# A maxout FFN behind local-window attention on one core: the output matmuls spread over the next chunk, two chunks of 256 tokens, another load order

## The chip, the core and the metric

The kernel runs on one core of a Trainium2 chip. A core has a matrix engine (TensorE, PE in the profile; its weight loads are shown apart as PEld), three engines for the rest (VectorE, DVE; ScalarE, ACT; GpSimd, POOL), and a queue engine that issues transfers (SyncE, SP). Each runs its own list of instructions in the order in which the program gave them, and waits for the others through semaphores. Data lie in SBUF, matmul results in the eight banks of PSUM. The metric is the device time of one execution in microseconds (us).

## The reference

There are 4 batches, 8 heads, 768 positions and head dimension 64. Each position sees the 96 last positions (itself included) and the first 8 positions of its sequence, with a bias that falls linearly with the distance. The attention output, 3072 tokens of 512 numbers, goes through a feed-forward network (FFN) with the maximum of three products:

```python
scores = scale * np.matmul(q, k.transpose(0, 1, 3, 2))
keep = is_global | is_local
dist = np.where(is_global & ~is_local, float(n_local), np.abs(rel).astype(np.float32))
scores = scores + (-slopes[:, None, None] * dist[None, :, :])[None, :, :, :]
scores = np.where(keep, scores, -1000000000.0)
a = np.exp(scores - np.max(scores, axis=-1, keepdims=True))
a = a / (np.sum(a, axis=-1, keepdims=True) + 1e-09)
x = np.matmul(a, v).transpose(0, 2, 1, 3).reshape(B * S, H * D)
h = np.maximum(np.maximum(x @ w1, x @ w2), x @ w3)   # 512 -> 768
return h @ w_out                                      # 768 -> 512
```

## The kernel before

The 3072 tokens are 24 tiles of 128 (six to a batch). Tile T is worked on in units, which are functions of the kernel:

- `load(T)` issues three transfers on SP (q, k, v of 256 KB each) into one of four buffers `raw`.
- `cast(T)` makes bf16 of q and k (L102) and of v (L104) on POOL. v stands in `va`, with a column of ones behind each head.
- `u_X(T)`, **X**: eight transposes on PE (L130) into the PSUM tile `tp`, and the copy to SBUF, `qkT`, on DVE (L132). Then POOL makes `kgT` (this tile's keys with the batch's first eight put in, L123 and L124) and `vg` (the same for v, L112 and L113), which the next tile uses as its second block of keys.
- `u_S(T, g)`, **S**, for half g of the heads: scores on PE into `sp` (L146), the exponential on ACT (L152, for the first tile of a batch L154). The product with the mask of biases, on DVE (L153, L155), is put off to the start of the next attention unit.
- `u_A(T, g)`, **A**: probabilities times v on PE into `op` (L166, L169); on DVE the reciprocal of the sum (L175) and the product with it (L176) into `xb`.
- `u_XT(T)`, **T**: four transposes of `xb` on PE into the same bank as `tp` (L187), and a copy on DVE into `xT` (L188).

The FFN goes by chunks of four tiles (512 tokens). `u_F1(c, f, j)`, **F1**, gives 128 of the 768 hidden numbers for product j: four matmuls into one bank `h0`, `h1` or `h2` (L199). For j = 0 ACT copies the bank (L204); for j = 1 and 2 DVE takes the maximum (L206, L208), the last into `ht`. `u_F2(c, tt)`, **F2**, gives the output of one tile: six matmuls into the bank `po` (L214), a copy on ACT into `ost` (L217), a store on SP (L219). A chunk is 18 F1 and then its four F2.

`load_w(g)` loads a third of the three weights (three transfers of 512 KB; here w0, w1, w2 for the groups), `cast_w(g)` makes bf16 of the three parts: w1's on ACT, w2's on DVE, w3's on POOL (L241 to L243).

What sets the order is the order in which the program emits units, and it is written by hand. The list `att` holds the attention units of all tiles. First `att` runs up to T(3), the last tile of chunk 0. Then, for each chunk c, F1 and F2 are emitted in turn, and between them the attention units of chunk c + 1, evenly. Per tile `att` has this order, which puts X of the next tile and T of the tile before side by side, and X(5) ahead of T(3):

```python
for i in range(NTT + 1):
    # S(i,0), A(i-1,1), S(i,1), X(i+1), T(i-1), A(i,0)
```

The loads are issued when the units ask for them, in the order tiles 0 to 3, w0, w1, w2, tile 4, w_out, tile 5, and on; X(T) asks for tile T + 3. Each of the PSUM tiles `tp`, `op`, `po`, `h0`, `h1`, `h2` is one bank and `sp` two; none has a second buffer.

Of the kernel before, what the change touches and what calls it, by code (L numbers as in the profile page):

```python
# [19 lines left out]
def kernel(  # L20
# [56 lines left out]
    NVA = 4  # L77
    va_ring = [persist.tile([128, H, 65], BF16, name=f"va{i}") for i in range(NVA)]
    va_first = [persist.tile([128, H, 65], BF16, name=f"vaf{i}") for i in range(2)]
    vg_ring = [persist.tile([128, H, 65], BF16, name=f"vg{i}") for i in range(3)]  # L80
    kg8 = [persist.tile([128, NP, NG], BF16, name=f"kg8_{i}") for i in range(2)]
# [4 lines left out]
    xT = {}  # L86
    va, vg = {}, {}

    def load(T):
# [7 lines left out]
    def cast(T):  # L97
        b, t = divmod(T, NT)
        r = raw[T]
        qk = cast_pool.tile([128, 2, DM], BF16, name="qkb", tag="qkb")  # L100
        qb[T] = qk
        nc.gpsimd.tensor_copy(qk, r[:, 0:2].rearrange("p a h d -> p a (h d)"))  # L102
        va[T] = va_first[b % 2] if t == 0 else va_ring[T % NVA]
        nc.gpsimd.tensor_copy(va[T][:, :, 0:D], r[:, 2])  # L104

    def make_vg(T):
        b, t = divmod(T, NT)
        if t == 0:
            vg[T] = va[T]
        elif t < NT - 1:  # L110
            vg[T] = vg_ring[T % 3]
            nc.gpsimd.tensor_copy(vg[T], va[T])  # L112
            nc.gpsimd.tensor_copy(vg[T][0:NG], va[b * NT][0:NG])  # L113

    def make_kg(T):
        b, t = divmod(T, NT)
        kT = qkT[T][:, 1]
        if t == 0:
            kgT[T] = kT
            nc.gpsimd.tensor_copy(kg8[b % 2], kT[:, :, 0:NG])  # L120
        elif t < NT - 1:
            kgT[T] = kg_pool.tile([128, NP, 128], BF16, name="kgT", tag="kgT")
            nc.gpsimd.tensor_copy(kgT[T], kT)  # L123
            nc.gpsimd.tensor_copy(kgT[T][:, :, 0:NG], kg8[b % 2])  # L124

    def u_X(T):
        tp = psT.tile([128, 2, NP, 128], BF16, name="tp", tag="tp")
        for a in range(2):
            for jp in range(NP):
                nc.tensor.transpose(tp[:, a, jp], qb[T][:, a, jp * 128:(jp + 1) * 128], identb)  # L130
        qkT[T] = qkT_pool.tile([128, 2, NP, 128], BF16, name="qkT", tag="qkT")
        nc.vector.tensor_copy(qkT[T], tp)  # L132
        make_kg(T)
        make_vg(T)
        return []

    def u_S(T, g):
        b, t = divmod(T, NT)
        sp = psS.tile([128, 2, 2, 2, 128], FP32, name="sp", tag="sp")
        for ds in range(2 if t else 1):  # L140
            for j2 in range(2):
                jp = 2 * g + j2
                for hh in range(2):
                    hsl = slice(64 * hh, 64 * hh + 64)
                    st = qkT[T][hsl, 1, jp] if ds == 0 else kgT[T - 1][hsl, jp]
                    nc.tensor.matmul(sp[:, hh, j2, ds], st, qkT[T][hsl, 0, jp],  # L146
                                     start=True, stop=True, skip_group_check=True)
        P = p_pool.tile([128, 4, 2, 128], BF16, name="P", tag="P")
        Pt[T, g] = P
        spv = sp.rearrange("p a b d n -> p (a b) d n")  # L150
        if t:
            nc.scalar.activation(P, spv, AF.Exp, bias=0.0, scale=scale)  # L152
            return [lambda: nc.vector.tensor_mul(P, P, wmask[:, g])]  # L153
        nc.scalar.activation(P[:, :, 0], spv[:, :, 0], AF.Exp, bias=0.0, scale=scale)  # L154
        return [lambda: nc.vector.tensor_mul(P[:, :, 0], P[:, :, 0], wmask0[:, g])]  # L155

    def u_A(T, g):
        b, t = divmod(T, NT)
        op = psO.tile([128, 4, 65], FP32, name="op", tag="op")
        P = Pt[T, g]  # L160
        for j2 in range(2):
            for hh in range(2):
                h = 4 * g + 2 * j2 + hh
                i = 2 * hh + j2
                o = op[:, 2 * j2 + hh]
                nc.tensor.matmul(o, P[:, i, 0], va[T][:, h], start=True, stop=(t == 0),  # L166
                                 skip_group_check=True)
                if t:
                    nc.tensor.matmul(o, P[:, i, 1], vg[T - 1][:, h], start=False, stop=True,  # L169
                                     skip_group_check=True)  # L170
        if g == 0:
            xb[T] = xb_pool.tile([128, H, D], BF16, name="xb", tag="xb")
        x = xb[T]
        rz = z_pool.tile([128, 4], FP32, name="rz", tag="rz")
        nc.vector.reciprocal(rz, op[:, :, 64])  # L175
        nc.vector.tensor_tensor(out=x[:, 4 * g:4 * g + 4], in0=op[:, :, 0:64],  # L176
                                in1=rz[:, :, None].to_broadcast([128, 4, D]), op=ALU.mult)
        return []

    def u_XT(T):  # L180
        c, i = divmod(T, CHUNK)
        if i == 0:
            xT[c] = xT_pool.tile([128, NP, CHUNK * 128], BF16, name="xT", tag="xT")
        tp = psT.tile([128, NP, 128], BF16, name="xtp", tag="tp")
        x = xb[T].rearrange("p h d -> p (h d)")
        for jp in range(NP):
            nc.tensor.transpose(tp[:, jp], x[:, jp * 128:(jp + 1) * 128], identb)  # L187
        nc.vector.tensor_copy(xT[c][:, :, i * 128:(i + 1) * 128], tp)  # L188
        return []
# [3 lines left out]

    def u_F1(c, f, j):
        if f == 0 and j == 0:
            ht[c] = ht_pool.tile([128, NF, CHUNK * 128], BF16, name="ht", tag="ht")
        ps = psH.tile([128, CHUNK * 128], FP32, name=f"h{j}", tag=f"h{j}")
        for dm in range(4):
            nc.tensor.matmul(ps, w123[f // 2][:, dm, j, (f % 2) * 128:(f % 2) * 128 + 128],  # L199
                             xT[c][:, dm], start=(dm == 0), stop=(dm == 3))  # L200
        if j == 0:
            h01 = h01_pool.tile([128, CHUNK * 128], BF16, name="h01", tag="h01")
            h01s[c, f] = h01
# [44 lines left out]
    with tc.manual_schedule():  # L248
# [4 lines left out]
        for tvar in va_ring + va_first:  # L253
            nc.vector.memset(tvar[:, :, 64:65], 1.0)
        BIGD = 60000.0
# [33 lines left out]
        tile_pos = {1: 1, 2: 2, 3: 3, 4: 7}  # L289
        for T in range(5, NTT):  # L290
            tile_pos[T] = T + 4
        done = [0]

        def loads_to(n):
            while done[0] < min(n, len(loads)):
                loads[done[0]]()
                done[0] += 1

        def upto(T):
            if T in tile_pos:  # L300
                loads_to(tile_pos[T])


        att = []
        att.append(("P", -1))
        for i in range(NTT + 1):
            if i < NTT:
# [12 lines left out]
        deferred = []  # L320
# [9 lines left out]
        def emit_att(u):  # L330
            tick()
            if u[0] == "P":
                upto(1)
                cast(0)
                upto(2)
                cast(1)
                u_X(0)
                upto(3)
            elif u[0] == "S":
                for fn in u_S(u[1], u[2]):  # L340
# [14 lines left out]
        def att_until(stop):  # L355
            nonlocal pos
            while pos < len(att):
# [3 lines left out]
                if u == stop:  # L361
                    break

        att_until(("T", chunks[0][-1]))
        cast_w(0)
        for c in range(NCH):
            ffn = [(u_F1, (c, f, j)) for f in range(NF) for j in range(3)]
            ffn += [(u_F2, (c, tt)) for tt in range(CHUNK)]
            if c + 1 < NCH:
                stop = ("T", chunks[c + 1][-1])  # L370
                end = att.index(stop) + 1
            else:
                end = len(att)
            n = end - pos
            slots = len(ffn) - 2
# [48 lines left out]
```

## Time and profile before

| | us |
|---|---|
| Time, median of 3 runs | 241.61 (241.36 to 242.32) |
| Profiled execution, its own time | 241.87 |
| Its span in the trace | 240.1 |
| ACT busy | 90.6 (38% of the span) |
| POOL busy | 78.6 (33%) |
| Read from memory / written | 25.17 MB / 6.29 MB |

In the profile's page each engine's span is cut into 40 slices of 6 us, with a digit for the busy share in tenths. A row of a group gives line, engine, operation, what it writes and reads, shapes, how often, busy us, mean ns of one, and how long the engine sat idle ahead of these instructions and for whom. A row of a timeline gives the start and the length in us, the instruction, and in brackets the wait ahead of it and who ended it.

### The profile page before, as it was taken

The numbers are of one execution on the slowest core, as the hardware profiler recorded it, in microseconds if no ns is written. First come the engines' busy times: TensorE is split into PE (matmuls) and PEld (weight loads), VectorE is DVE, ScalarE is ACT, GpSimd is POOL, SyncE is SP. The second block draws the span as 40 slices with busy tenths as digits, with TensorE's granted clock in tenths as the row PEclk, the third lists the DMA queues.
The fourth block names the chain that finished last, engine by engine and source line by source line (L and its number), as shares of the span: only waits on it lengthen the run. The fifth ranks groups of instructions, "written<-read, shape, count | busy, mean of one in ns | idle before, by whom it ended". The sixth has DMA issues, their size and how long they took to land. (4 is left out here: it accounts for less than half of the span.)

```text
span 240.1 us, 4041 instructions
## 1 busy us (share of the span) xinstructions
PE 188.0 (78%) x1568; PEld 98.2 (41%) x1568; DVE 134.3 (56%) x278; ACT 90.6 (38%) x131; POOL 78.6 (33%) x131
## 2 busy tenths in 40 slices
PE   0556215598889898987998877999879889889972
PEld 0435113354444454543554534544434445334420
DVE  1567405468776187771687671878734776524510
ACT  6533304063565435422643423434424335122111
POOL 4577123624534326025065440215550500000000
PEclk9999999999999999999999999999999999999999
DMA  8999999999601988208896009990022000130022
GB/s 158 218 249 349 347 245 278 224 219 218 126 4 46 247 198 180 35 0 184 227 161 134 0 26 238 228 210 3 0 87 90 0 3 0 63 113 3 0 86 90
DMA packets 83923, 31.72 MB, mean 132 GB/s; under 512 B 75456, under 2 KB 80064, under 8 KB 83904
## 3 DMA queue, kind: packets, MB, share of 16 engines
q1 hardware_dynamic: 83904, 31.46, 58.2%
q8 instruction: 12, 0.20, 0.3%
q14 instruction: 7, 0.06, 0.1%
HBM read 25.17 MB, written 6.29 MB: 131 GB/s over the span
## 5 line engine op out<-in xcount | busy, mean ns | idle before, releaser
L199 PE MATMUL h<-xT,w 128*128 128x512 bf16 x432 | 109.9, 384 | 0.5 <-DVE xT L188 0.5
L152 ACT ACTIVATE P<-sp 128x1024 bf16<-128x1024 f32 x40 | 41.0, 1024 | 49.1 <-PE sp L146 49.1
L199 PEld LDWEIGHTS <-w 128*128 128x128 bf16 x432 | 37.0, 98 | 35.6 <-issue 1.8
L214 PE MATMUL po<-wo,ht 128*128 128x512 bf16 x144 | 35.7, 379 | 11.0 <-ACT ost L217 9.5
L206 DVE TENSOR_TENSOR h<-h,h 128x512 bf16<-128x512 bf16 x36 | 24.7, 686 | 25.5 <-PE h L199 20.9
L204 ACT CAST h<-h 128x512 bf16<-128x512 f32 x36 | 21.1, 585 | 46.8 <-PE h L199 44.3
L153 DVE TENSOR_TENSOR P<-P,wmask 128x1024 bf16<-128x1024 bf16 x40 | 31.1, 778 | 5.9 <-ACT P L152 5.8
L130 PE MATMUL tp<-identb,qkb 128*128 128x128 bf16 x192 | 17.2, 242 | 19.4 <-POOL qkb L102 19.4
L123 POOL COPY kgT<-qkT 128x512 bf16<-128x512 bf16 x16 | 9.8, 613 | 64.8 <-DVE qkT L132 64.8
L102 POOL CAST qkb<-raw 128x1024 bf16<-128x1024 f32 x24 | 24.8, 1033 | 17.9 <-DMA raw<-in_k_dram 17.9
L217 ACT COPY ost<-po 128x512 f32<-128x512 f32 x24 | 14.0, 585 | 37.8 <-PE po L214 34.9
L208 DVE TENSOR_TENSOR ht<-h,h 128x512 bf16<-128x512 bf16 x36 | 24.6, 682 | 5.9 <-PE h L199 5.1
L214 PEld LDWEIGHTS <-ht 128*128 128x128 bf16 x144 | 13.6, 97 | 29.1 <-issue 13.0
L132 DVE COPY qkT<-tp 128x1024 bf16<-128x1024 bf16 x24 | 16.5, 686 | 16.0 <-PE tp L130 15.9
L130 PEld LDWEIGHTS <-qkb 128*128 128x128 bf16 x192 | 14.2, 109 | 24.4 <-POOL qkb L102 20.6
L175 DVE RECIPROCAL rz<-op 128x4 f32<-128x4 f32 x48 | 8.5, 176 | 25.0 <-PE op L169 20.2
L176 DVE TENSOR_TENSOR xb<-op,rz 128x256 bf16<-128x256 f32 x48 | 20.4, 424 | 1.7
L187 PE MATMUL xtp<-identb,xb 128*128 128x128 bf16 x96 | 10.0, 232 | 12.8 <-DVE qkT L132 12.8
L166 PEld LDWEIGHTS <-P 128*128 128x128 bf16 x192 | 15.5, 105 | 9.5 <-DVE xb L176 5.0
L146 PE MATMUL sp<-qkT 64*128 64x128 bf16 x224 | 16.0, 238 | 3.7 <-ACT P L152 1.7
L166 PE MATMUL op<-va,P 128*128 128x65 bf16 x160 | 16.5, 203 | 0.7 <-DVE xb L176 0.7
L187 PEld LDWEIGHTS <-xb 128*128 128x128 bf16 x96 | 8.0, 104 | 20.5 <-issue 17.4
(42 smaller groups left out, 137.6 us busy)
## 6 DMA issues: line engine op xcount, KB each, us to landing
raw<-in_q_dram SPq DMA_DIRECT2D x24, 256.0 KB, 4.7
raw<-in_k_dram SPq DMA_DIRECT2D x24, 256.0 KB, 5.0
raw<-in_v_dram SPq DMA_DIRECT2D x24, 256.0 KB, 4.9
out_dram<-ost SPq DMA_DIRECT2D x24, 256.0 KB, 2.2
wst<-in_moe_w_dram SPq DMA_DIRECT2D x9, 512.0 KB, 8.4
wst<-in_moe_w_out_dram SPq DMA_DIRECT2D x3, 512.0 KB, 6.0
```

Source lines behind the costliest of these rows:

```text
L102: nc.gpsimd.tensor_copy(qk, r[:, 0:2].rearrange("p a h d -> p a (h d)"))
L130: nc.tensor.transpose(tp[:, a, jp], qb[T][:, a, jp * 128:(jp + 1) * 128], identb)
L152: nc.scalar.activation(P, spv, AF.Exp, bias=0.0, scale=scale)
L153: return [lambda: nc.vector.tensor_mul(P, P, wmask[:, g])]
L166: nc.tensor.matmul(o, P[:, i, 0], va[T][:, h], start=True, stop=(t == 0), skip_group_check=True)
L176: nc.vector.tensor_tensor(out=x[:, 4 * g:4 * g + 4], in0=op[:, :, 0:64], in1=rz[:, :, None].to_broadcast([128, 4, D]), op=ALU.mult)
L187: nc.tensor.transpose(tp[:, jp], x[:, jp * 128:(jp + 1) * 128], identb)
L199: nc.tensor.matmul(ps, w123[f // 2][:, dm, j, (f % 2) * 128:(f % 2) * 128 + 128], xT[c][:, dm], start=(dm == 0), stop=(dm == 3))
L204: nc.scalar.copy(h01, ps)
L206: nc.vector.tensor_max(h01s[c, f], h01s[c, f], ps)
L208: nc.vector.tensor_max(ht[c][:, f], h01s[c, f], ps)
L214: nc.tensor.matmul(po, ht[c][:, f, tt * 128:(tt + 1) * 128], wo[:, f], start=(f == 0), stop=(f == NF - 1))
```

## The change

Six things change.

1. **Chunks**: their sizes are 4, 2, 2, 4, 4, 4, 4 tiles, so chunks 1 and 2 have 256 tokens. The banks and matmuls of F1 are then half as wide.
2. **F2 in the next chunk**: the F2 of chunk c - 1 are emitted between the F1 of chunk c, one behind each f from 1 on. The last chunk's F2 stay at its end.
3. **Order of attention**: in the first four tiles each tile's units follow one another (X, A of the tile before, S, S, T). Later, T(i-1) stands behind A(i,0) and not directly behind X(i+1); T(3) stands behind X(4) and not X(5).
4. **Loads**: order tiles 0 to 3, w0, w1, tile 4, w2, tile 5, w_out; X(T) asks for tile T + 5; `raw` has six buffers.
5. **Copies**: X's copy of q and k goes from DVE to ACT. POOL's copies for `kgT` and `vg` read and write the same bytes as 32-bit words, half as many.
6. **PSUM banks of the first four tiles**: X of odd tiles uses the bank `h2`, S of the second half of the heads `h0` and `h1` (the exponential is then two instructions), A of the second half `po`.

```diff
-    CHUNK = 4
-    chunks = [list(range(c, c + CHUNK)) for c in range(0, NTT, CHUNK)]
+    sizes = [4, 2, 2, 4, 4, 4, 4]
...
+    NSTART = sizes[0]
-    raw_pool = ctx.enter_context(tc.tile_pool(name="raw", bufs=4))
+    raw_pool = ctx.enter_context(tc.tile_pool(name="raw", bufs=6))
...
+    def words(ap):
+        return ap.bitcast(mybir.dt.int32)
...
-            nc.gpsimd.tensor_copy(vg[T], va[T])
-            nc.gpsimd.tensor_copy(vg[T][0:NG], va[b * NT][0:NG])
+            nc.gpsimd.tensor_copy(words(vg[T]), words(va[T]))
+            nc.gpsimd.tensor_copy(words(vg[T][0:NG]), words(va[b * NT][0:NG]))
...
-            nc.gpsimd.tensor_copy(kgT[T], kT)
+            nc.gpsimd.tensor_copy(words(kgT[T]), words(kT))
...
     def u_X(T):
-        tp = psT.tile([128, 2, NP, 128], BF16, name="tp", tag="tp")
+        if T < NSTART and T % 2:
+            tp = psH.tile([128, 2, NP, 128], BF16, name="tph", tag="h2")
+        else:
+            tp = psT.tile([128, 2, NP, 128], BF16, name="tp", tag="tp")
...
-        nc.vector.tensor_copy(qkT[T], tp)
+        nc.scalar.copy(qkT[T], tp)
...
     def u_S(T, g):
+        alt = T < NSTART and g == 1
+        if alt:
+            sps = [psH.tile([128, 2, 2, 128], FP32, name=f"sph{hh}", tag=f"h{hh}")
+                   for hh in range(2)]
...
     def u_A(T, g):
+        if T < NSTART and g == 1:
+            op = psP.tile([128, 4, 65], FP32, name="opp", tag="po")
...
     def u_F1(c, f, j):
+        W = len(chunks[c]) * 128
...
-        ps = psH.tile([128, CHUNK * 128], FP32, name=f"h{j}", tag=f"h{j}")
+        ps = psH.tile([128, W], FP32, name=f"h{j}", tag=f"h{j}")
...
-        loads = [lambda T=T: load(T) for T in range(1, 4)]
-        loads += [lambda g=g: load_w(g) for g in range(3)]
-        loads += [lambda: load(4), load_wo] + [lambda T=T: load(T) for T in range(5, NTT)]
+        loads = [("T", T) for T in range(1, NSTART)] + [("w", 0), ("w", 1), ("T", NSTART),
+                                                        ("w", 2), ("T", NSTART + 1), ("o",)]
+        loads += [("T", T) for T in range(NSTART + 2, NTT)]
...
+        for i in range(NSTART):
+            att.append(("X", i))
+            if i >= 1:
+                att += [("A", i - 1, 0), ("A", i - 1, 1)]
+            att += [("S", i, 0), ("S", i, 1)]
+            if i >= 1:
+                att.append(("T", i - 1))
+        i = NSTART - 1
+        att += [("A", i, 0), ("X", i + 1), ("A", i, 1), ("S", i + 1, 0), ("T", i)]
+        for i in range(NSTART, NTT + 1):
+            if i < NTT and i > NSTART:
                 att.append(("S", i, 0))
-            if i >= 1:
+            if i > NSTART:
                 att.append(("A", i - 1, 1))
             if i < NTT:
                 att.append(("S", i, 1))
             if i + 1 < NTT:
                 att.append(("X", i + 1))
-            if i >= 1:
-                att.append(("T", i - 1))
             if i < NTT:
                 att.append(("A", i, 0))
+            if i > NSTART:
+                att.append(("T", i - 1))
...
-                upto(T + 3)
+                upto("T", T + 5)
...
-            ffn = [(u_F1, (c, f, j)) for f in range(NF) for j in range(3)]
-            ffn += [(u_F2, (c, tt)) for tt in range(CHUNK)]
+            ffn = []
+            for f in range(NF):
+                ffn += [(u_F1, (c, f, j)) for j in range(3)]
+                if c and f >= 1 and f <= len(chunks[c - 1]):
+                    ffn.append((u_F2, (c - 1, f - 1)))
             if c + 1 < NCH:
...
                 end = len(att)
+                ffn += [(u_F2, (c, tt)) for tt in range(len(chunks[c]))]
```

On SP the change reorders the first loads. Before, from the last part of weight group w1 on (`raw_261` is tile 4, `raw_331` tile 5, the last three `wst` are w_out):

```order
L230 DMA wst_253<-in_moe_w3_dram 128x4x256
L230 DMA wst_255<-in_moe_w1_dram 128x4x256
L230 DMA wst_257<-in_moe_w2_dram 128x4x256
L230 DMA wst_259<-in_moe_w3_dram 128x4x256
L95 DMA raw_261<-in_q_dram 128x8x64
L95 DMA raw_261<-in_k_dram 128x8x64
L95 DMA raw_261<-in_v_dram 128x8x64
L237 DMA wst_325<-in_moe_w_out_dram 128x2x512
L237 DMA wst_327<-in_moe_w_out_dram 128x2x512
L237 DMA wst_329<-in_moe_w_out_dram 128x2x512
L95 DMA raw_331<-in_q_dram 128x8x64
```

The same place on SP after the change (`raw_220` is tile 4, `raw_230` tile 5):

```order
L262 DMA wst_218<-in_moe_w3_dram 128x4x256
L108 DMA raw_220<-in_q_dram 128x8x64
L108 DMA raw_220<-in_k_dram 128x8x64
L108 DMA raw_220<-in_v_dram 128x8x64
L262 DMA wst_224<-in_moe_w1_dram 128x4x256
L262 DMA wst_226<-in_moe_w2_dram 128x4x256
L262 DMA wst_228<-in_moe_w3_dram 128x4x256
L108 DMA raw_230<-in_q_dram 128x8x64
L108 DMA raw_230<-in_k_dram 128x8x64
L108 DMA raw_230<-in_v_dram 128x8x64
L269 DMA wst_271<-in_moe_w_out_dram 128x2x512
```

Tile 4 now stands ahead of weight group w2, and tile 5 ahead of w_out.

On POOL, where the FFN begins, before the change (`raw_331` is tile 5, `raw_410` tile 6, `w123_0` and `w123_1` the parts of w3 in groups w0 and w1):

```order
L102 CAST qkb_485<-raw_331 128x1024
L104 CAST va1_115<-raw_331 128x8x64
L102 CAST qkb_558<-raw_410 128x1024
L104 CAST vaf1_119<-raw_410 128x8x64
L243 CAST w123_0_125<-wst_247 128x4x256
L243 CAST w123_1_126<-wst_253 128x4x256
```

On POOL after the change (`raw_230` is tile 5, `raw_277` tile 6):

```order
L115 CAST qkb_520<-raw_230 128x1024
L117 CAST va1_115<-raw_230 128x8x64
L275 CAST w123_0_125<-wst_212 128x4x256
L115 CAST qkb_597<-raw_277 128x1024
L117 CAST vaf1_119<-raw_277 128x8x64
L275 CAST w123_1_126<-wst_218 128x4x256
```

w3's first cast no longer stands behind tile 6, but still behind tile 5; its second stands behind tile 6.

On ACT, at the end of chunk 0 before the change (`ost` is the copy of an F2, `h01` that of an F1, `P` an exponential):

```order
L152 ACTIVATE P_959<-sp_950 128x1024
L217 COPY ost_968<-po_961 128x512
L217 COPY ost_1002<-po_995 128x512
L217 COPY ost_1018<-po_1011 128x512
L217 COPY ost_1028<-po_1021 128x512
L204 CAST h01_1037<-h0_1032 128x512
L152 ACTIVATE P_1061<-sp_1052 128x1024
```

On ACT within chunk 3 after the change (`qkT` is X's copy of q and k):

```order
L178 ACTIVATE P_1720<-sp_1711 128x1024
L249 COPY ost_1748<-po_1741 128x512
L178 ACTIVATE P_1760<-sp_1751 128x1024
L148 COPY qkT_1772<-tp_1763 128x1024
L236 CAST h01_1791<-h0_1786 128x512
L178 ACTIVATE P_1833<-sp_1824 128x1024
L249 COPY ost_1855<-po_1848 128x512
L178 ACTIVATE P_1867<-sp_1858 128x1024
```

The copies of the F2 no longer follow one another, and X's copy stands in ACT's list behind the exponential of the S before it.

More of the change, by code (lines that the diff above doesn't have):

```diff
@@ L47 @@
     slopes = [2.0 ** (-8.0 * (h + 1) / H) for h in range(H)]
-    CHUNK = 4
-    chunks = [list(range(c, c + CHUNK)) for c in range(0, NTT, CHUNK)]
+    sizes = [4, 2, 2, 4, 4, 4, 4]
+    assert sum(sizes) == NTT
+    chunks, where = [], {}
+    for n in sizes:
+        first = chunks[-1][-1] + 1 if chunks else 0
+        for i in range(n):
+            where[first + i] = (len(chunks), i)
+        chunks.append(list(range(first, first + n)))
     NCH = len(chunks)
+    NSTART = sizes[0]
     persist = ctx.enter_context(tc.tile_pool(name="persist", bufs=1))
-    raw_pool = ctx.enter_context(tc.tile_pool(name="raw", bufs=4))
+    raw_pool = ctx.enter_context(tc.tile_pool(name="raw", bufs=6))
     cast_pool = ctx.enter_context(tc.tile_pool(name="cast", bufs=3))
@@ L77 @@
     NVA = 4
-    va_ring = [persist.tile([128, H, 65], BF16, name=f"va{i}") for i in range(NVA)]
-    va_first = [persist.tile([128, H, 65], BF16, name=f"vaf{i}") for i in range(2)]
-    vg_ring = [persist.tile([128, H, 65], BF16, name=f"vg{i}") for i in range(3)]
+    va_ring = [persist.tile([128, H * 65], BF16, name=f"va{i}") for i in range(NVA)]
+    va_first = [persist.tile([128, H * 65], BF16, name=f"vaf{i}") for i in range(2)]
+    vg_ring = [persist.tile([128, H * 65], BF16, name=f"vg{i}") for i in range(3)]
     kg8 = [persist.tile([128, NP, NG], BF16, name=f"kg8_{i}") for i in range(2)]
@@ L138, in u_S @@
         b, t = divmod(T, NT)
-        sp = psS.tile([128, 2, 2, 2, 128], FP32, name="sp", tag="sp")
+        alt = T < NSTART and g == 1
+        if alt:
+            sps = [psH.tile([128, 2, 2, 128], FP32, name=f"sph{hh}", tag=f"h{hh}")
+                   for hh in range(2)]
+        else:
+            sp = psS.tile([128, 2, 2, 2, 128], FP32, name="sp", tag="sp")
+            sps = [sp[:, hh] for hh in range(2)]
         for ds in range(2 if t else 1):
@@ L145, in u_S @@
                     st = qkT[T][hsl, 1, jp] if ds == 0 else kgT[T - 1][hsl, jp]
-                    nc.tensor.matmul(sp[:, hh, j2, ds], st, qkT[T][hsl, 0, jp],
+                    nc.tensor.matmul(sps[hh][:, j2, ds], st, qkT[T][hsl, 0, jp],
                                      start=True, stop=True, skip_group_check=True)
@@ L180, in u_XT @@
     def u_XT(T):
-        c, i = divmod(T, CHUNK)
+        c, i = where[T]
         if i == 0:
-            xT[c] = xT_pool.tile([128, NP, CHUNK * 128], BF16, name="xT", tag="xT")
+            xT[c] = xT_pool.tile([128, NP, len(chunks[c]) * 128], BF16, name="xT", tag="xT")
         tp = psT.tile([128, NP, 128], BF16, name="xtp", tag="tp")
@@ L201, in u_F1 @@
         if j == 0:
-            h01 = h01_pool.tile([128, CHUNK * 128], BF16, name="h01", tag="h01")
+            h01 = h01_pool.tile([128, W], BF16, name="h01", tag="h01")
             h01s[c, f] = h01
@@ L283, with upto @@
                                  scale=-slopes[h])
[L286 to L307 removed]
+        loads = [("T", T) for T in range(1, NSTART)] + [("w", 0), ("w", 1), ("T", NSTART),
+                                                        ("w", 2), ("T", NSTART + 1), ("o",)]
+        loads += [("T", T) for T in range(NSTART + 2, NTT)]
+        done = [0]
+        def upto(*what):
+            if what[0] == "T" and what[1] >= NTT:
+                return
+            while what in loads[done[0]:]:
+                x = loads[done[0]]
+                done[0] += 1
+                if x[0] == "T":
+                    load(x[1])
+                elif x[0] == "w":
+                    load_w(x[1])
+                else:
+                    load_wo()
+        att = []
+        for i in range(NSTART):
[9 more added lines that the diff above has]
+            if i < NTT and i > NSTART:
                 att.append(("S", i, 0))
[L309 removed]
+            if i > NSTART:
                 att.append(("A", i - 1, 1))
@@ L331, in emit_att @@
             tick()
[L332 to L339, printed above, removed]
+            if u[0] == "S":
                 for fn in u_S(u[1], u[2]):
@@ L362, in att_until @@
                     break
+        upto("T", 3)
+        cast(0)
         att_until(("T", chunks[0][-1]))
```

30 lines of the change are left out of this document (19 added, 11 removed).

## The prediction

> **What bounds the kernel now.** I read the page first. TensorE (PE) is by far the busiest engine, but in its forty slices of 6 us it is thin at the start, where the DMA engines are full.
>
> ```profile
> PE 188.0 (78%) x1568; PEld 98.2 (41%) x1568; DVE 134.3 (56%) x278; ACT 90.6 (38%) x131; POOL 78.6 (33%) x131
> ...
> PE   0556215598889898987998877999879889889972
> ...
> DMA  8999999999601988208896009990022000130022
> ```
>
> So the span has two parts: up to slice 8 (48 us) PE waits for something, behind it PE is nearly full. Next I read PE's timeline for the moment at which the FFN begins. L130 is unit X (transposes of q and k), L199 is F1, one bank of the first FFN layer.
>
> ```profile
> 35.31 1.03 PE L130 MATMUL tp<-identb,qkb 128*128 128x128 bf16 x8 [9.01 <-POOL qkb L102]
> ...
> 46.33 1.86 PE L199 MATMUL h<-xT,w 128*128 128x512 bf16 x4 [0.52 <-DVE xT L188]
> ...
> 49.11 1.70 PE L199 MATMUL h<-xT,w 128*128 128x512 bf16 x4
> ...
> 50.89 1.03 PE L199 MATMUL h<-xT,w 128*128 128x512 bf16 x4
> ...
> 59.22 1.04 PE L199 MATMUL h<-xT,w 128*128 128x512 bf16 x4
> ...
> 60.09 0.61 PE L130 MATMUL tp<-identb,qkb 128*128 128x128 bf16 x8
> ```
>
> The first row is X(4), which waited 9 us; then come the 1st, 2nd, 3rd and 9th F1 of chunk 0, and X(7). What X waits for stands in the timeline of GpSimd (POOL):
>
> ```profile
> 34.21 1.04 POOL L102 CAST qkb<-raw 128x1024 bf16<-128x1024 f32 x1 [9.08 <-DMA raw<-in_k_dram]
> ...
> 37.21 0.61 POOL L123 COPY kgT<-qkT 128x512 bf16<-128x512 bf16 x1 [1.40 <-DVE qkT L132]
> 37.88 0.21 POOL L124 COPY kgT<-kg 128x32 bf16<-128x32 bf16 x1
> ...
> 42.32 1.04 POOL L102 CAST qkb<-raw 128x1024 bf16<-128x1024 f32 x1 [3.00 <-DMA raw<-in_k_dram]
> ...
> 45.77 1.04 POOL L102 CAST qkb<-raw 128x1024 bf16<-128x1024 f32 x1 [1.77 <-DMA raw<-in_k_dram]
> 46.86 0.96 POOL L104 CAST vaf<-raw 128x512 bf16<-128x512 f32 x1
> 47.77 1.03 POOL L243 CAST w<-wst 128x1024 bf16<-128x1024 f32 x1
> ```
>
> The three casts at 34.21, 42.32 and 45.77 are tiles 4, 5 and 6, each started when its load landed. The last row is POOL's third of the first weight group (w3), which the third F1 needs; it stood in the queue behind tile 6. Behind 60 us, the waits of PE (us, times, longest) are these:
>
> ```profile
> PE po L214 <- ACT ost L217: 9.5, 17, 1.0
> PE xtp L187 <- DVE qkT L132: 7.7, 13, 1.0
> PE po L214 <- DVE ht L208: 1.4, 2, 1.1
> ```
>
> F2 (L214) waits for the one bank `po` that the copy of the F2 before still reads; T (L187) waits for the one bank `tp` that X's copy still reads. Rates and a middle chunk come from the windows view (us; busy PE, PEld, DVE, ACT, POOL; clock; DMA share; GB/s), the end from the chain of waits and from the waits of L214 behind 229 us:
>
> ```profile
> 24.00:30.00 6.00, 1.80 (x25) 1.20 (x24) 2.56 (x7) 2.05 (x2) 1.07 (x2) 1.00 1.10 347
> 48.00:60.00 12.00, 11.31 (x101) 5.79 (x100) 8.73 (x19) 5.95 (x9) 4.52 (x6) 1.00 1.18 218
> 147.30:180.00 32.70, 29.89 (x258) 15.11 (x257) 21.04 (x44) 13.01 (x18) 12.37 (x21) 1.00 0.56 117
> ```
>
> ```profile
> 212.59 15.54 PE h L199 x72
> ```
>
> ```profile
>   ACT ost L217: 2.4, 3
> ```
>
> A middle chunk takes 32.7 us. Eighteen F1 without a gap take 15.54: 0.86 each, 216 ns a matmul, so six matmuls of F2 take 1.3. Of the 32.7, the waits above are (7.7 + 9.5 - 2.4 + 1.4) / 5 = 3.2; 15.5 + 4 x 1.3 is FFN, and 8.8 is left for 24 attention units, 0.36 each.
>
> **Start of the FFN.** The load queue does not empty before slice 10, so the new order changes only which load comes when. Weights move at 347 GB/s (24 to 30 us), tiles at 218 (48 to 60): a tile of 0.786 MB takes 3.6 us, a weight group of 1.573 MB 4.5. Four tiles and about 1.6 us of start are in by 16.0; then w0 and w1 by 25.0, tile 4 by 28.6, w2 by 33.1, tile 5 by 36.7. For before, the same sum (all weights to 29.5, tile 4 to 33.1) is 1.1 early against the cast at 34.2; I add 0.6: **tile 4 at 29.2, tile 5 at 37.3** (ends 0 and 1.1). Tile 6 has the same bytes ahead of it as before and stays at 45.8.
>
> From tile 4: cast 1.04, X 1.03, copy on ACT 1.02, S(4,0) at most X's 1.03, its exp 1.02, and behind that ACT's cast of w1, like the other casts 1.04. The first F1 starts at 35.4 (before 46.3); with S(4,1), a second F1 of 1.70 and X(5), whose cast ends at 38.3, PE comes to the third F1 at about 40.5. Its w3 stands behind tile 5 on POOL: 37.3 + 1.04 + 0.96 + 1.03 = 40.3. So the third starts at 40.5 instead of 50.9. Units 3 to 7 with four attention units are 5.8 us, to 46.3; X(6) waits for tile 6's cast to 46.8; the second w3 cast is ready at 45.8 + 1.04 + 0.96 + 1.03 = 48.8. **The ninth F1 starts at 49.0 instead of 59.2.** By then four units that were done before are still to come, T(4), S(6,0), A(5,1), S(6,1), two of them half-size: +1.1. **Term A = -10.2 + 1.1 = -9.1** (ends -7.5, with tile 5 later, and -11, with tile 6 1.9 earlier).
>
> The extra banks, split exponentials and 32-bit copies of the first four tiles I cost at nothing: before, PE had done all ahead of X(4) by 35.31 - 9.01 = 26.3, and X(4) can't start before 30.2. Without that cover each would count by a part of a us per tile. The deeper prefetch costs nothing either: loads are issued five tiles ahead, one or two more than now, so a store that waits in front of one on SP has a chunk's time.
>
> **F2 spread.** Between two F2 stand at least three F1 (1.3 us even with 256 tokens), against about 0.7 us from an F2's end to the next one's start in the last rows ((2.4 - 1.0) / 2). Only the last four F2 stay together and keep their 2.4. An F2 in the next chunk also finds `ht` ready. **Term B = -(9.5 - 2.4) - 1.4 = -8.5** (ends -6.5, if ACT's queue makes some copies late, and -8.5).
>
> **q/k copies on ACT, T behind A.**
>
> ```profile
> L152 ACT ACTIVATE P<-sp 128x1024 bf16<-128x1024 f32 x40 | 41.0, 1024 | 49.1 <-PE sp L146 49.1
> ...
> L204 ACT CAST h<-h 128x512 bf16<-128x512 f32 x36 | 21.1, 585 | 46.8 <-PE h L199 44.3
> ...
> L132 DVE COPY qkT<-tp 128x1024 bf16<-128x1024 bf16 x24 | 16.5, 686 | 16.0 <-PE tp L130 15.9
> ```
>
> No row shows this copy on ACT. Between DVE's 0.69 and 1.17 (twice L204's 0.585) I take the exp's 1.02, same engine and size. ACT gets 24 x 1.02 = 24.5 us, 115 in all; DVE loses 16.5. Neither is full. The copy stands behind the exp of S(i,1). In chunks of 512 tokens, either two F1 lie between X and T or one there and one ahead of X: counted from the end of S(i,1) the exp ends at 1.1, the copy at 2.2, and PE comes to T at 0.5 + 2 x 0.86 + 0.36 = 2.6, without a wait. In chunk 2 (256 tokens, attention of four tiles beside it) F1 is half as long, PE comes at 1.7 and waits 0.5, for four tiles 2.0. **Term C = -7.7 + 2.0 = -5.7** (ends 0, if the copy is as late as DVE's was, and -7.7).
>
> **256-token chunks.** 144 matmuls become 288 of half the columns. Warm, X's eight take 0.61 with some 0.2 for the last one's way out, 56 ns apart for 128 columns; 512 take 216. That is 0.417 ns a column and 2.7 ns a matmul: 109 ns for 256, +0.4 us in all. In chunk 2 PE has 7.9 + 2 x 1.3 + 8.8 = 19.3 us of work, 4.8 a tile. Beside it runs a loop: X 0.5, ACT's copy 1.02, four POOL copies, the cast 1.04, signals 0.4. A 32-bit copy of 256 words lies between the rows of 0.21 and 0.61; I take 0.4, so the loop is 4.4. That is near PE's 4.8, and each S waits for the exp of the S before (one pair of banks). I take 2.5 us of new waits for chunks 1 and 2, ends 0 and 6. **Term D = +2.9.**
>
> **Sum.** 240.1 - 9.1 - 8.5 - 5.7 + 2.9 = 219.7. The profiled execution took 241.87, 1.77 over its span and 0.26 over the median of 241.61: 219.7 + 1.77 - 0.26 = **221.2**.
>
> **Rivals.**
> (1) *ACT's copy is as late as DVE's was* and chunks 1 and 2 wait more: C = 0, D = 5, so 227.5 + 1.5 = **229**. For it: 1.02 instead of 0.69, behind an exp. Against it: the F1 and A that now lie between X and T.
> (2) *PE runs slowly longer.* F1 goes from 1.70 to 1.03 some 4 us after PE got busy at 46. If the wait for tile 6 or 5 brought the slow rate back up to the ninth F1, six F1 would each take 0.84 more, 5.0: **226**. Waits of up to 1.1 us did not do that behind 60 us.
> The Trainium skill, "TensorE: Matmul & The Clock Gate", Part 1, lets the clock fall to half after an idle window of about 3.4 us. By it my waits, under 2 us, would not cool PE and this rival falls; the trace agrees as far as the slow F1 at 49.11 stand behind long waits and the fast ones behind 4 busy us.
> (3) *Slower: ACT gates every tile.* If X's copy stood behind an exp and an h copy each time, T would come 1.02 + 0.59 + 1.02 - 0.36 - 0.86 = 1.4 us late; 20 tiles make 28 us in place of 7.7, 240.1 - 9.1 - 8.5 + 20.3 + 2.9 = 245.7, **247**. From 1.1 us a tile on it is slower than before. Against it: in ACT's new order the h copy stands behind the q/k copy, and ACT was 38% busy.
> (4) *The start gains less*: tiles 5 and 6 land later, since loads share the engines, and w3's casts with them. With A = -4: **226**.
>
> **Chances.** Forecast 0.68 (own range 217 to 225), (1) 0.13, (2) 0.05, (3) 0.04, (4) 0.10. The low end, 217, takes the better ends of A and C; the high end, 229, takes in (1), (2) and (4). A measurement of this kernel tells about 0.5% from no change. Faster by more 0.95, within 0.02, slower 0.03.
>
> **What would show it.** First, third and ninth F1 at 35, 40 and 49 us, with POOL waiting for raw data ahead of the w3 cast; F2's waits down to the last three; T's waits for ACT under 3 us and in chunk 2; a 512-token chunk in 29 to 30 us. It is wrong if ACT leads PE's waits, or if F1 rows of 1.70 stand behind 42 us.

## The result and the profile after

| | before | changed |
|---|---|---|
| Time, median | 241.71 us (241.36 to 242.32) | 216.78 us (216.41 to 217.42) |
| Span of the profiled execution | 240.1 us | 214.9 us |

The ratio is 0.897, with an interval of 0.894 to 0.900. The kernel is 10.3% faster; 221.2 was predicted, with a range down to 217.0. So the way was right, but the gain that was forecast was too small by 4.4 us, and 216.78 lies 0.2 us below the range. The page of the changed kernel, the same rows as before:

```profile
PE 182.7 (85%) x1640; PEld 103.1 (48%) x1640; DVE 121.5 (57%) x266; ACT 113.0 (53%) x165; POOL 66.1 (31%) x131
...
PE   0446825998999999789999999999999999999962
...
DMA  7999999999999894889547980111101111012122
```

A slice is now 5.4 us. PE is full from slice 7 (38 us) on, 10 us sooner, and from there to the last two slices one slice is under 8, where before it had four. Next comes PE's timeline at the start of the FFN (X(4), then the 1st, 2nd, 3rd and 9th F1):

```profile
30.78 1.03 PE L146 MATMUL tp<-identb,qkb 128*128 128x128 bf16 x8 [4.00 <-POOL qkb L115]
...
35.75 1.86 PE L231 MATMUL h<-xT,w 128*128 128x512 bf16 x4 [1.64 <-DVE xT L219]
...
38.09 1.89 PE L231 MATMUL h<-xT,w 128*128 128x512 bf16 x4
...
40.42 1.03 PE L231 MATMUL h<-xT,w 128*128 128x512 bf16 x4
...
49.30 1.04 PE L231 MATMUL h<-xT,w 128*128 128x512 bf16 x4 [1.16 <-POOL w L275]
```

And POOL's timeline at the same place, the casts of tiles 4, 5 and 6 and w3's first two:

```profile
29.68 1.04 POOL L115 CAST qkb<-raw 128x1024 bf16<-128x1024 f32 x1 [4.62 <-DMA raw<-in_k_dram]
...
37.64 1.04 POOL L115 CAST qkb<-raw 128x1024 bf16<-128x1024 f32 x1 [3.19 <-DMA raw<-in_k_dram]
38.68 0.62 POOL L117 CAST va<-raw 128x512 bf16<-128x512 f32 x1
39.24 1.04 POOL L275 CAST w<-wst 128x1024 bf16<-128x1024 f32 x1
...
45.31 1.04 POOL L115 CAST qkb<-raw 128x1024 bf16<-128x1024 f32 x1 [5.03 <-DMA raw<-in_k_dram]
47.64 0.62 POOL L117 CAST vaf<-raw 128x512 bf16<-128x512 f32 x1 [1.29 <-DMA raw<-in_v_dram]
48.20 1.04 POOL L275 CAST w<-wst 128x1024 bf16<-128x1024 f32 x1
```

Predicted were 35, 40 and 49 us for the three F1, and loads of tiles 4, 5 and 6 at 29.2, 37.3 and 45.8. The ninth F1 waits for w3's second cast, that one for v of tile 6. The start is as forecast. Now PE's waits from 49 us on:

```profile
PE po L246 <- ACT ost L249: 2.2, 3, 0.7
PE op L197 <- DVE xb L207: 1.5, 2, 1.2
PE xtp L218 <- ACT qkT L148: 1.5, 3, 0.8
PE h L231 <- POOL w L275: 1.2, 1, 1.2
PE sp L168 <- ACT P L178: 0.7, 3, 0.4
PE h L231 <- DVE ht L240: 0.3, 1, 0.3
```

F2's waits are down to the last three and T's to 1.5 us, also as forecast: 6.2 us of waits without the one for w3, where the sum had 2.4 + 2.0 + 2.5 = 6.9. What is not as forecast is the middle chunk. From the first F2 inside chunk 4 to the first one inside chunk 5 the windows view has

```profile
134.50:162.70 28.20, 27.97 (x251) 14.63 (x248) 17.53 (x39) 16.42 (x22) 9.62 (x21) 1.00 0.10 39
```

28.2 us instead of 32.7, and instead of the 29 to 30 that were forecast. PE's waits in the middle chunk before, from 147.30 to 180.00 us, are

```profile
PE po L214 <- ACT ost L217: 2.2, 4, 0.7
PE xtp L187 <- DVE qkT L132: 1.3, 3, 0.7
```

That is 3.5 us (the prediction's account, an average over the chunks, had 3.2); one wait of 0.2 is left in the chunk after. So 4.5 us left the chunk, where the wait rows hold 3.3.

### The profile page after: what moved, and what is told of

Same layout as the page of the kernel before. It is cut to its first block, busy times and chain, and to the rows that moved or that the text cites. A ratio compares the mean times of both kernels' runs of the same rounds, so it can differ in the third digit from the quotient of the medians.

```text
span 214.9 us, 4230 instructions
## 1 busy us (share of the span) xinstructions
PE 182.7 (85%) x1640; PEld 103.1 (48%) x1640; DVE 121.5 (57%) x266; ACT 113.0 (53%) x165; POOL 66.1 (31%) x131
## 4 chain that ended last, share of the span: by engine, by line
PE 60%; SPq 17%; ACT 10%; DMA 4%; DVE 4%; issue 2%; POOL 1%; ACTq 0%
PE h L231 35%; PE po L246 14%; SPq L108 13%; ACT P L178 5%; DMA raw<-in_v_dram 4%; PE sp L168 4%; SPq L262 3%; DVE P L182 3%; PE xtp L218 2%; ACT qkT L148 2%; PE tp L146 2%; PE op L197 2%; ACT h L236 1%; ACT ost L249 1%; PE op L200 1%
## 5 line engine op out<-in xcount | busy, mean ns | idle before, releaser
L231 PE MATMUL h<-xT,w 128*128 128x512 bf16 (+1 forms) x504 | 110.7, 353 | 3.1 <-DVE xT L219 1.6
L231 PEld LDWEIGHTS <-w 128*128 128x128 bf16 x504 | 44.0, 98 | 35.9 <-issue 1.8
L178 ACT ACTIVATE P<-sp 128x1024 bf16<-128x1024 f32 (+1 forms) x44 | 42.1, 958 | 21.6 <-PE sp L168 21.6
L238 DVE TENSOR_TENSOR h<-h,h 128x512 bf16<-128x512 bf16 (+1 forms) x42 | 25.5, 608 | 29.0 <-PE h L231 28.4
L236 ACT CAST h<-h 128x512 bf16<-128x512 f32 (+1 forms) x42 | 22.2, 528 | 22.5 <-PE h L231 22.2
L148 ACT COPY qkT<-tp 128x1024 bf16<-128x1024 bf16 x22 | 22.3, 1014 | 13.2 <-PE tp L146 13.2
L240 DVE TENSOR_TENSOR ht<-h,h 128x512 bf16<-128x512 bf16 (+1 forms) x42 | 25.5, 608 | 5.2 <-PE h L231 3.3
L146 PE MATMUL tp<-identb,qkb 128*128 128x128 bf16 x176 | 14.9, 234 | 13.6 <-POOL qkb L115 10.7
L146 PEld LDWEIGHTS <-qkb 128*128 128x128 bf16 x192 | 13.8, 108 | 19.8 <-POOL qkb L115 14.7
L197 PEld LDWEIGHTS <-P 128*128 128x128 bf16 x192 | 15.0, 103 | 7.7 <-DVE xb L207 2.3
L168 PEld LDWEIGHTS <-qkT 64*128 64x128 bf16 x224 | 7.6, 101 | 19.5 <-issue 15.7
L200 PEld LDWEIGHTS <-P 128*128 128x128 bf16 x160 | 12.2, 103 | 2.4
L117 POOL CAST va<-raw 128x512 bf16<-128x512 f32 x20 | 12.7, 635 | 0.1
```

The costliest lines, as they stand in the source:

```text
L148: nc.scalar.copy(qkT[T], tp)
L168: nc.tensor.matmul(sps[hh][:, j2, ds], st, qkT[T][hsl, 0, jp], start=True, stop=True, skip_group_check=True)
L178: nc.scalar.activation(P[:, :, 0:n], sp.rearrange("p a b d n -> p (a b) d n")[:, :, 0:n], AF.Exp, bias=0.0, scale=scale)
L197: nc.tensor.matmul(o, P[:, i, 0], heads(va[T])[:, h], start=True, stop=(t == 0), skip_group_check=True)
L238: nc.vector.tensor_max(h01s[c, f], h01s[c, f], ps)
L240: nc.vector.tensor_max(ht[c][:, f], h01s[c, f], ps)
```

## The experiments

The theory after the result: a wait of PE costs more than its row. A matmul's row is longer than the distance to the next one (512 columns: 0.38 against 0.22 us), and an idle row begins at the end of that longer row. So each wait hides 0.38 - 0.22 = 0.16 us more. The rival: the rows hold the whole cost, and the rest comes from an edit that was priced wrongly.

**Single parts put into the kernel before.** First F2's order alone:

```diff
-            ffn = [(u_F1, (c, f, j)) for f in range(NF) for j in range(3)]
-            ffn += [(u_F2, (c, tt)) for tt in range(CHUNK)]
+            ffn = []
+            for f in range(NF):
+                ffn += [(u_F1, (c, f, j)) for j in range(3)]
+                if c and f >= 1 and f <= CHUNK:
+                    ffn.append((u_F2, (c - 1, f - 1)))
+            if c + 1 == NCH:
+                ffn += [(u_F2, (c, tt)) for tt in range(CHUNK)]
```

> The kernel before, with only the F2 of each chunk moved into the next one. Theory (a wait costs more than its idle row: the row starts at the modelled end of the last matmul, 0.16 us after the next could have started): 13 of the 17 waits for the copy and one or two for ht go, 9.5 - 2.4 + 1.4 = 8.5 us of idle rows and 15 x 0.16 = 2.4 us with them, so 10 to 11.5 us faster than before, a time of 230 to 231.5. Rival (the rows give the whole cost, and the extra gain of the change comes from elsewhere): 8.0 to 8.7 faster, 233 to 233.6. T's waits stay as in the kernel before, about 7 us behind 60 us.

233.04 us, ratio 0.961 (0.959 to 0.964), span 231.3. By the time alone this is the rival's. The waits view behind 50 us:

```profile
PE xtp L187 <- DVE qkT L132: 8.6, 15, 1.2
PE po L214 <- ACT ost L217: 2.2, 3, 0.7
PE op L166 <- DVE xb L176: 2.0, 2, 1.7
```

F2's rows fell as expected, but a new wait of 2.0 us for `op` came up, which neither side had. Over the whole span the PE wait rows fall from 48.1 to 41.9, 6.2 us, in 40 waits instead of 54, and the span falls by 8.8: 6.2 + 14 x 0.16 = 8.4. The time didn't decide; the balance of the trace speaks for the theory.

T's place alone:

```diff
-            if i >= 1:
-                att.append(("T", i - 1))
             if i < NTT:
                 att.append(("A", i, 0))
+            if i >= 1:
+                att.append(("T", i - 1))
```

> The kernel before, with only T(i-1) moved behind A(i,0); X's copy stays on VectorE. Theory: T's 13 waits behind 60 us (7.7 us of rows) fall to under 1.5 us, and each takes 0.16 us more with it, so 7.5 to 9.5 us faster, 232 to 234; F2's waits stay at 9 to 10 us. Rival (the copy has to leave VectorE for the wait to go): T still waits 4 us or more and the time falls by less than 4 us, to 238 or above.

233.38 us, ratio 0.964 (0.961 to 0.967), span 231.5. T's waits behind 50 us:

```profile
PE xtp L187 <- DVE qkT L132: 0.2, 1, 0.2
```

A hit: in the order of the kernel before, T's place is enough, with the copy on DVE. The span falls by 8.6 us, all wait rows by 7.4 (48.1 to 40.7) in 14 fewer waits; with 0.16 for each that would be 9.6.

**Single parts taken out of the changed kernel.** The copy back on DVE:

```diff
-        nc.scalar.copy(qkT[T], tp)
+        nc.vector.tensor_copy(qkT[T], tp)
```

> The changed kernel, with X's copy back on VectorE. Theory (the order removed T's wait, not the engine): within 1% of the changed kernel, 215 to 219. Rival (the gain beyond the forecast comes from work that leaves VectorE): T's and F1's waits for VectorE come back, 4 us or more slower, 221 or above.

220.88 us, ratio 0.912 (0.909 to 0.915): a miss, 4.1 us slower than the changed kernel and at the rival's edge. In the changed order the engine does matter: T waits 4.2 us for DVE in 6 waits, instead of 1.5 us for ACT in 3. Against the changed kernel the first F2 inside chunk 1 starts 0.4 us later, the first inside chunk 3 2.9 and the first inside chunk 4 4.0 (138.59 for 134.54); from there on the distance stays. So most of it is lost in chunks 1 and 2, where much attention stands beside short F1, but 1.1 us in chunk 3, whose F1 are not short.

Chunks of four tiles throughout, `sizes = [4, 4, 4, 4, 4, 4]`:

> The changed kernel with six chunks of four tiles. Theory (256-token chunks cost waits and give nothing that is needed): the waits of the narrow chunks (about 3.5 us of rows between 58 and 98 us) and 0.4 us of matmul floor go, 212.5 to 215. Rival (they are needed so that the first chunk doesn't wait for tiles 6 and 7): chunk 0 waits for loads or for T(7) and X(9), 2 to 5 us slower than the changed kernel, 219 to 222.

216.69 us, ratio 0.895 (0.892 to 0.897): neither, the same time as the changed kernel. Waits behind 50 us are 4.3 us in all, but the ninth F1 starts at 53.4 instead of 49.3 with 27 attention units in chunk 0 instead of 15. In this pair the narrow chunks give up about what they gain.

Both together:

```diff
-    sizes = [4, 2, 2, 4, 4, 4, 4]
+    sizes = [4, 4, 4, 4, 4, 4]
...
-        nc.scalar.copy(qkT[T], tp)
+        nc.vector.tensor_copy(qkT[T], tp)
```

> The changed kernel with six chunks of four tiles and X's copy on VectorE. Theory (the copy's engine matters only in the narrow chunks, where attention is packed and VectorE is full; in 512-token chunks the order is enough): 216 to 218, as with the copy on ScalarE. Rival (ScalarE's copy is worth 4 us everywhere): 220 to 222.

220.88 us, ratio 0.913 (0.910 to 0.915): again a miss, the copy on DVE costs 4.2 us without narrow chunks too. But not in the last chunks: against the uniform kernel with ACT's copy, the first F2 inside chunk 1 starts at 79.5 for 76.6, the first inside chunk 3 at 138.8 for 134.5, and from there to the first inside chunk 4 it takes 28.0 us with DVE's copy and 28.2 with ACT's. What is slow is chunk 0, whose 18 F1 carry 27 attention units (T waits 3.1 us for DVE there, against 0.5 for ACT in the uniform kernel; A waits 1.2 in both), with another us lost before chunk 3. Of the 4.1 us of span, 2.1 are wait rows and 0.6 the hidden part of 4 more waits; 1.4 us stay open.

Everything undone but the start:

```diff
-    sizes = [4, 2, 2, 4, 4, 4, 4]
+    sizes = [4, 4, 4, 4, 4, 4]
...
-        nc.scalar.copy(qkT[T], tp)
+        nc.vector.tensor_copy(qkT[T], tp)
...
-                if c and f >= 1 and f <= len(chunks[c - 1]):
-                    ffn.append((u_F2, (c - 1, f - 1)))
...
-                ffn += [(u_F2, (c, tt)) for tt in range(len(chunks[c]))]
+            ffn += [(u_F2, (c, tt)) for tt in range(len(chunks[c]))]
...
+            if i > NSTART:
+                att.append(("T", i - 1))
             if i < NTT:
                 att.append(("A", i, 0))
-            if i > NSTART:
-                att.append(("T", i - 1))
```

> The changed kernel with everything but the start undone: six chunks of four tiles, F2 at the end of its own chunk, X's copy on VectorE, T(i-1) directly behind X(i+1); kept are the load order, the six buffers, the order of the first four tiles with their banks, and the 32-bit copies. Theory (the start alone is worth what the prediction gave it, 9.1 us): first F1 near 36, time 231.5 to 234. Rival (the earlier start is given back, since loads of tiles 6 to 9 or the narrow chunks' absence hold up chunk 0): less than 5 us faster than before, 236.5 or above.

235.09 us, ratio 0.972 (0.969 to 0.975): between the two. The first F1 starts at 36.0 and the third at 42.4 instead of 40.4. The start alone gives 7.3 us of span on uniform chunks.

Without the banks of the first tiles and the 32-bit words:

```diff
-        return ap.bitcast(mybir.dt.int32)
+        return ap
...
-        if T < NSTART and T % 2:
+        if False:
...
-        alt = T < NSTART and g == 1
+        alt = False
...
-        if T < NSTART and g == 1:
+        if False:
```

> The changed kernel without the extra PSUM banks of the first four tiles and without the 32-bit copies on GpSimd. Theory (cover: PE waits for tile 4 anyway): 216 to 218, tile 4's cast still starts on its load near 29.7. Rival (they are part of the gain beyond the forecast): 219 or above.

216.01 us, ratio 0.893 (0.891 to 0.895): a hit. Tile 4's cast starts at 30.11. These two edits are worth nothing that can be measured here.

F2 back at the end of its own chunk:

```diff
-                if c and f >= 1 and f <= len(chunks[c - 1]):
-                    ffn.append((u_F2, (c - 1, f - 1)))
...
-                ffn += [(u_F2, (c, tt)) for tt in range(len(chunks[c]))]
+            ffn += [(u_F2, (c, tt)) for tt in range(len(chunks[c]))]
```

> The changed kernel with each chunk's F2 back at its own end. Theory (each of 12 to 16 waits of 0.3 to 0.72 us comes back with 0.16 more): 8 to 11 us slower than the changed kernel, 225 to 228. Rival (part of what F2's spreading gave was the start's or the copy's): 5 us slower or less, 222 or below.

230.61 us, ratio 0.953 (0.951 to 0.955): 13.8 us slower, more than either. All PE wait rows are 40.1 us in 43 waits instead of 28.1 in 25: 12.0 + 18 x 0.16 = 14.9, against 14.2 of span. That looks closer than it is: PE's slow time after one of the waits (last section) makes about another 1.7 us by the granted clock, so that the balance is some 2.4 us too high, and why is open. F2's own rows make 10.4 + 0.7 instead of 2.2; with fewer attention units between the F1, PE also waited 2.3 us for w3's second cast, after which the slow time came, and once 2.0 us for A.

**The price of one wait.** The second and third of the last four F2 get banks that are free by then:

```diff
-        po = psP.tile([128, DM], FP32, name="po", tag="po")
+        if c == NCH - 1 and tt in (1, 2):
+            po = psH.tile([128, DM], FP32, name="poh", tag=f"h{tt - 1}")
+        else:
+            po = psP.tile([128, DM], FP32, name="po", tag="po")
```

> The changed kernel with the second and third of the last four F2 in the banks h0 and h1. Theory (a wait costs its row and 0.16 us more): the three waits of 0.72 us go and the starts of the last four F2 lie 1.3 us apart instead of 2.17, 3 x 0.87 = 2.6 us in all, 213.8 to 214.4. Rival (the row is the whole cost): 2.2 us, and the starts still lie 1.45 apart, 214.4 to 214.8.

214.63 us, ratio 0.888 (0.885 to 0.890): by time the rival's. By the distance of the starts, which PE's timeline shows directly, it is the theory's; first the changed kernel,

```profile
203.07 1.46 PE L246 MATMUL po<-wo,ht 128*128 128x512 bf16 x6
205.25 1.46 PE L246 MATMUL po<-wo,ht 128*128 128x512 bf16 x6 [0.72 <-ACT ost L249]
207.42 1.46 PE L246 MATMUL po<-wo,ht 128*128 128x512 bf16 x6 [0.72 <-ACT ost L249]
209.59 1.46 PE L246 MATMUL po<-wo,ht 128*128 128x512 bf16 x6 [0.72 <-ACT ost L249]
```

and with the two banks (the second row holds two F2):

```profile
203.82 1.46 PE L249 MATMUL po<-wo,ht 128*128 128x512 bf16 x6
205.11 2.75 PE L249 MATMUL poh<-wo,ht 128*128 128x512 bf16 x12
207.70 1.46 PE L249 MATMUL po<-wo,ht 128*128 128x512 bf16 x6
```

From the first to the last of the four it is 6.52 us before and 3.88 after, 2.64 less, where the rows show 3 x 0.72 = 2.16. Each wait hid 0.16 us more. (The span fell by 1.9, since this execution came to the first of them 0.75 us later.) With the other load order, further down, the same two banks take the time from 212.71 to 209.92, 2.8 us.

The same holds over all kernels. In this table the rows of all PE waits are summed over the whole span, and taken off it:

| kernel | span | PE wait rows | waits | span less rows |
|---|---|---|---|---|
| before | 240.1 | 48.1 | 54 | 192.0 |
| start alone | 232.8 | 41.6 | 47 | 191.2 |
| F2 at its chunk's end | 229.1 | 40.1 | 43 | 189.0 |
| F2 spread alone | 231.3 | 41.9 | 40 | 189.4 |
| T behind A alone | 231.5 | 40.7 | 40 | 190.8 |
| copy on DVE | 218.9 | 30.7 | 29 | 188.2 |
| uniform, copy on DVE | 218.9 | 30.3 | 27 | 188.6 |
| changed kernel | 214.9 | 28.1 | 25 | 186.8 |
| without banks and words | 214.0 | 26.8 | 25 | 187.2 |
| two tail banks | 213.0 | 27.7 | 25 | 185.3 |
| other load order | 210.1 | 24.7 | 24 | 185.4 |
| uniform | 214.8 | 28.2 | 23 | 186.6 |
| load order and tail banks | 208.3 | 22.5 | 23 | 185.8 |
| the same, uniform | 210.7 | 23.0 | 22 | 187.7 |

If rows were the whole cost and the kernels differed in nothing else, the last column would not depend on the number of waits. A straight line through the 14 gives 182.3 us plus 0.18 us a wait, and the scatter falls from 2.1 to 1.0 us. The line was drawn after the runs, and the kernels do differ in more than their waits, so it supports the theory and doesn't prove it; the starts of the last four F2 are the direct measurement.

**Versions that go on from here.** Another load order, by the same reading of the queue:

```diff
-        loads = [("T", T) for T in range(1, NSTART)] + [("w", 0), ("w", 1), ("T", NSTART),
-                                                        ("w", 2), ("T", NSTART + 1), ("o",)]
+        loads = [("T", T) for T in range(1, NSTART)] + [("w", 0), ("T", 4), ("w", 1), ("T", 5),
+                                                        ("T", 6), ("w", 2), ("T", 7), ("o",)]
...
```

> The changed kernel with the loads in the order tiles 0 to 3, w0, tile 4, w1, tiles 5, 6, w2, tile 7, w_out. Theory (up to the ninth F1 the landing of tiles 4, 5 and 6 sets the time, each by its place in the queue): tile 4's cast near 25, tile 5's near 33, tile 6's near 37, first F1 near 31, ninth near 43 to 44, 4 to 6 us faster than the changed kernel, 210.5 to 213. Rival (another limit stands close behind: PE's own work from tile 4 on, or the casts of w1 and w3): 2 us or less faster, 214.5 or above.

212.71 us, ratio 0.880 (0.878 to 0.882): a hit. PE's timeline has the first, third and ninth F1 at

```profile
32.22 1.87 PE L231 MATMUL h<-xT,w 128*128 128x512 bf16 x4 [1.63 <-DVE xT L219]
...
36.41 1.03 PE L231 MATMUL h<-xT,w 128*128 128x512 bf16 x4
...
43.63 1.02 PE L231 MATMUL h<-xT,w 128*128 128x512 bf16 x4
```

The ninth comes 5.7 us sooner than in the changed kernel, and the time falls by 4.1. This order and the two tail banks together:

> The changed kernel with the other load order and the two banks for the last F2 together. Theory: the start and the tail don't meet, so the gains add, 4.1 + 2.6 us: 209.5 to 211. Rival (the tail is bound by the stores, not by PE): no faster than the load order alone, 212 to 213.

**209.92 us, ratio 0.867 (0.866 to 0.869)**: a hit, the fastest of all versions. The same on uniform chunks:

> The same two edits on six chunks of four tiles. Theory (narrow chunks give up in waits what they gain in chunk 0, as in the changed kernel): within 1 us of the version with narrow chunks. Rival (with earlier loads chunk 0 no longer waits for attention of tiles 6 and 7): 1.5 to 3 us faster than with narrow chunks.

212.59 us, ratio 0.877 (0.873 to 0.881): 2.7 us slower, outside both. With the early loads, X waits once for 2.9 us in chunk 0, and PE is slow behind that. Here the narrow chunks pay.

## Why the prediction was right and wrong

- **Start (term A, -9.1)**: right. The ninth F1 came 9.9 us earlier; less the four units that were still to do, 1.1, that is 8.8. The casts of tiles 4, 5 and 6 started within 0.5 us of the times worked out. The load-order run shows the mechanism, since moving tiles 5 and 6 ahead in the queue moved the ninth F1. Rival (4) is out for the changed kernel; on uniform chunks the start is worth 7.3.
- **F2 spread (B, -8.5)**: the waits named went, 9.5 + 1.4 us of rows to 2.2. The price of them was too small (see the sum).
- **Copy on ACT, T behind A (C, -5.7)**: T's rows fell by 6.2. The reason given was half right. T's place is enough in the order of the kernel before, but in the changed one the copy on DVE costs 4.1 us; the prediction credited the copy's engine with nothing. Rivals (1) and (3), which feared ACT, are out: ACT is 53% busy, and T waits 1.5 us for it.
- **256-token chunks (D, +2.9)**: the new waits for A, S and `ht` are 2.5 us behind 49 us, as large as forecast, but that was in part luck: the uniform kernel has 1.6 of them too (A 1.2, S 0.4), so the narrow chunks are not their only cause. Nor are these chunks a net cost, since the uniform kernel takes the same time: it has fewer waits, but its ninth F1 comes 4.1 us later.
- **Cover of the first tiles' edits**: right, by the run without banks and words.
- **The sum**: this is the step that failed. Terms B and C priced each wait by its idle row, "-(9.5 - 2.4) - 1.4" and "-7.7 + 2.0". The same reading gave "8.8 is left for 24 attention units, 0.36 each", which put the hidden part of the waits into the attention's work, where it seemed bound to stay. A middle chunk of 28.2 us less 15.5 and 5.2 of FFN leaves 7.5. Each wait cost 0.16 us more than its row. Behind the ninth F1 the kernel before has 33 waits, the changed one 12: 21 x 0.16 = 3.4 us of the 219.7 - 214.9 = 4.8 us that are missing. The rows themselves fell by 12.6 us (18.8 to 6.2) where B, C and D had 11.7, 0.9 more; A gave 0.3 less. The last 0.8 us stay open. The 4.1 us that the copy's engine is worth are not a second account of the gap, since the sum already had T's waits on ACT at 2.0 us and 1.5 came; but work that left DVE may be in the 0.8, since with the copy on DVE rows and hidden parts leave 0.8 us open in the changed kernel (4.0 of span less 2.6 and 0.6) and 1.4 in the uniform one. That these waits would go was right, the size of one wait was not. The needed rows stood in the prediction: an F1's row of 1.03 us beside 0.86 from start to start.
- **Rival (2)** did not come true in the changed kernel, whose longest wait after 40 us is 1.2 us, and in which no F1 row of 1.70 or more stands behind 42 us; PE did fall back to the slow rate in two experiments, below. ACT leads PE's waits behind 49 us, which was named as a sign of being wrong, but with the three waits for F2's copies that the sum had left in.

## What to carry to other kernels

Price a wait of PE from start to start, not by its idle row: take the distance between the two starts with the wait and without it, or add to every row what a single matmul's row has over the distance of matmuls in a stream (here 0.16 us at 512 columns). Where many short waits go, their number counts beside their sum. And where a queue of loads is never empty, add up the bytes ahead of each one: that gave the loads' times here within 0.5 us, and a better order.

## What the hardware showed that was not expected

A wait of 2.27 us was enough to slow PE. With F2 at its chunk's end, PE's timeline at w3's second cast is

```profile
50.02 1.04 PE L231 MATMUL h<-xT,w 128*128 128x512 bf16 x4 [2.27 <-POOL w L275]
50.89 0.77 PE L146 MATMUL tp<-identb,qkb 128*128 128x128 bf16 x8
51.45 1.91 PE L231 MATMUL h<-xT,w 128*128 128x512 bf16 x4
```

and the windows view has the granted clock (before the last two numbers) at

```profile
50.00:52.00 2.00, 1.98 (x14) 1.24 (x15) 0.91 (x2) 0.25 (x1) 0.95 (x1) 0.80 0.91 199
52.00:54.00 2.00, 2.00 (x13) 0.93 (x12) 1.14 (x3) 1.36 (x3) 1.18 (x3) 0.50 1.16 234
```

Idle for 2.27 us, PE first ran on at the full rate for about 1 us, and then at half. It had been busy before the wait, 1.95 us of the two from 44 us on and 1.75 of the next two. With the other load order on uniform chunks, PE was slow at once behind a wait of 2.87 us (an X of 1.03 us instead of 0.61):

```profile
54.68 1.03 PE L146 MATMUL tp<-identb,qkb 128*128 128x128 bf16 x8 [2.87 <-POOL qkb L115]
...
58.09 1.91 PE L231 MATMUL h<-xT,w 128*128 128x512 bf16 x4
```

In the same execution with F2 at its chunk's end, a wait only a little shorter slowed nothing; the F1 of 256 columns behind it take 0.60 us, as before it:

```profile
96.42 0.20 PE L197 MATMUL op<-va,P 128*128 128x65 bf16 x1 [2.03 <-DVE xb L207]
...
96.67 0.60 PE L231 MATMUL h<-xT,w 128*128 128x256 bf16 x4
```

Nor did the changed kernel's waits of up to 1.2 us behind 49 us slow PE. The Trainium skill, "TensorE: Matmul & The Clock Gate", Part 1, gives an idle window of about 3.4 us for this, and says that the window runs free of the kernel. The measurement decides here: 2.27 us was enough once, and 2.03 us another time was not. What sets the two apart, the length alone, the place of the wait in such a window or the work around it, no run here separates.

The record of the clock is no proof of the full rate. In the changed kernel the windows view shows 1.00 in the stretch in which the F1 at 38.09 took 1.89 us:

```profile
36.00:40.00 4.00, 4.00 (x19) 1.44 (x18) 0.30 (x1) 1.57 (x2) 2.36 (x3) 1.00 1.19 303
```

The lengths of the rows tell the rate more surely.
